# Experts on scaled f16 halves in place of fp32r halves, with range checks, wider weight pieces and work moved to GpSimd

## The chip, the cores and the metric

The kernel runs on one core of one Trainium2 chip. The metric is device time in microseconds. A core has TensorE (PE, its weight loads listed as PEld), VectorE (DVE), ScalarE (ACT), GpSimd (POOL), SyncE (SP, which only issues transfers here) and 16 DMA engines.

## The reference

Three parts follow one another. The first is bucketed attention: a query sees only the keys that have the same six sign bits. The second sends each of 1536 tokens to one of eight experts. The third is a dense layer pair with a hard gate.

```
q_bucket, k_bucket = six sign bits of q @ proj, k @ proj        # 16 heads, 768 positions, 64 wide
attn = softmax(where(q_bucket == k_bucket, q @ k.T / 8, -1e9))
x = (attn @ v) as 1536 tokens x 512
expert_idx = argmax(x @ w_gate); gate_w = its softmax value     # 8 experts, capacity 384 each
out[i] = gate_w[i] * (relu(x[i] @ w1[e]) @ w2[e])               # w1 512 x 1024, w2 1024 x 512
h = out @ w_in;  g = h * clip(h + 3, 0, 6) / 6                  # 512 -> 2048
result = g @ w_out                                              # 2048 -> 512
```

## The kernel before

The order of each engine's instructions is the order in which the Python code calls them; pools of buffers add the waits. Four stages stand one behind the other: attention, the routing with the first gather of tokens, the experts, and the last layer pair. Some work of the next stage is placed between the matmuls of the one that runs.

**Experts.** The loop in lines 1102 to 1148 runs over eight experts. Tokens of an expert are gathered from memory by POOL's queue into two tiles `xg` (`gather`, line 938), multiplied by their gate value (`scale_x`, line 945, DVE), transposed by PE and split by ACT and DVE into a high and a low half `xh`, `xl` (`make_x`, lines 954 to 958). An expert handles W = 224 columns of tokens. `gemm1` (line 971) has KF = 8 steps f of twelve matmuls: three products of halves (high with high, low with high, high with low) for four pieces of the inner dimension. ACT takes the high half of the result through Relu (`hh`, line 973), DVE the low one (`hl`, line 974). `gemm2` (line 997) has eight steps s of twelve matmuls; every second one ends with an eviction to `yTh` (ACT, line 1000) and `yTl` (DVE, line 1001), which are f16. All halves before that are fp32r. psh and psy have three PSUM buffers each.

**Weights.** `load_w` issues transfers of 512 KB on SP's queue into four buffers `rawp`. `split_w` halves them in pieces of 512 columns: `wh` on ACT (line 144), `wl` on DVE (line 145). Each expert has 16 such pieces; those of w2 are made in the steps of its own gemm1, those of w1 in the steps of the gemm2 ahead of it:

```
for f in range(KF):                                  # gemm1 of expert e
    split_w(wp2, e, 2 + f // 4, f % 4)
    if nxt and f % 2:
        load_w(e + 1, f // 4, (f // 2) % 2)
    gemm1(e, f)
    if 0 < e < 4:
        next(cgen, None)
    elif 3 < e < 7 and f % 2:
        zeros(4 * (e - 4) + f // 2)
```

**Beside them.** `compact` is a generator that computes indices with small DVE operations and a few matmuls; experts 1 to 3 take one item of it per step of gemm1. `zeros` (lines 981 and 983, ACT) writes zeros behind the tokens of each slot; experts 4 to 6 do four calls of two copies each. scale_x of the next expert stands at s = 2 and 3 of gemm2, make_x at s = 5 and 6.

**Last stage.** `up` (line 1190) and `down` (line 1217) work on f16 halves, the up weights being split into `ch` and `cl`. Sums of squares of the halves are collected through ACT's accumulator (line 1160), and `verdict` sets a flag when one of four sums is out of range; then a second branch computes the experts and the rest again in fp32. POOL scatters the result (line 1232).

Of the kernel before, what the change touches and what calls it, by code (L numbers as in the profile page):

```python
# [56 lines left out]
@with_exitstack
def moe_attention_kernel(ctx, tc, qk, v, vt, pj, wg, w1, w2, win, wout, out, cap):
# [43 lines left out]
    s8 = persist([P, 8], F32, "s8")  # L102
    f9 = persist([1, 9], F32, "f9")
# [20 lines left out]
    rawp = opened(wctx, "rawp", 4, side="right")  # L124
# [11 lines left out]
    def split_w(wp, e, i, q, lo=None):  # L136
        lo = lo or dve
        kind = "12"[i // 2]
        if q == 0:
            wh[e, i] = wp.tile([P, 2048], F32R, tag=f"wh{kind}", name=f"wh{e}_{i}")  # L140
            wl[e, i] = wp.tile([P, 2048], F32R, tag=f"wl{kind}", name=f"wl{e}_{i}")
        r = raw[e, i, q // 2][:, (q % 2) * 512 : (q % 2 + 1) * 512]
        c = slice(q * 512, (q + 1) * 512)
        act.activation(wh[e, i][:, c], r, AF.Copy)  # L144
        lo.tensor_tensor(out=wl[e, i][:, c], in0=r, in1=f32(wh[e, i])[:, c], op=ALU.subtract)  # L145
# [128 lines left out]
    with ExitStack() as actx:  # L274
# [668 lines left out]
    def scale_x(e, j):  # L943
        t = xg_t[e, j]
        dve.tensor_scalar(out=t, in0=t, scalar1=gates[:, e, j : j + 1], scalar2=None, op0=ALU.mult)

    def make_x(e, j):
        if j == 0:
            xs_t[e] = tuple(xp.tile([P, KD, W], F32R, tag=n, name=f"{n}{e}") for n in ("xh", "xl"))
        xh, xl = xs_t[e]  # L950
        t = xg_t.pop((e, j))
        ps = ps_a.tile([P, KD, P], F32, tag="a", name=f"psa{e}{j}")
        for k in range(KD):
            pe.transpose(ps[:, k], t[:, k * P : (k + 1) * P], ident)
        c = slice(j * GW, (j + 1) * GW)
        ps = ps[:, :, 0:GW]
        act.activation(xh[:, :, c], ps, AF.Copy)
        dve.tensor_tensor(out=xl[:, :, c], in0=ps, in1=f32(xh)[:, :, c], op=ALU.subtract)

    def gemm1(e, f):  # L960
        xh, xl = xs_t[e]
        if f == 0:
            h_t[e] = tuple(xp.tile([P, KF, W], F32R, tag=n, name=f"{n}{e}") for n in ("hh", "hl"))
# [9 lines left out]
        act.activation(hh[:, f], ps, AF.Relu)  # L973
        dve.scalar_tensor_tensor(out=hl[:, f], in0=ps, scalar=0.0, in1=f32(hh)[:, f], op0=ALU.max, op1=ALU.subtract)
# [12 lines left out]
    def gemm2(e, d, half, ra, rv):  # L987
# [114 lines left out]
    for e in range(E):  # L1102
# [45 lines left out]
    with ExitStack() as cctx:  # L1148
# [13 lines left out]
        def spans():  # L1162
            o = 2 * KG
            for i, (a, b) in enumerate(((0, o), (o, o + KG), (o + KG, o + 2 * KG), (o + 2 * KG, o + 2 * KG + KD))):
                dve.tensor_reduce(out=s8[:, i : i + 1], in_=sq[:, a:b], axis=AX.X, op=ALU.add)
            dve.tensor_scalar(out=s8[:, 4:8], in0=s8[:, 0:4], scalar1=TOP, scalar2=None, op0=ALU.is_le)

        def verdict():
            ps = ps_g.tile([P, 512], F32, tag="g", name="psr")
            pe.matmul(ps[0:1, 0:8], ones[:, 0:1], s8, start=True, stop=True)  # L1170
            for i, c in enumerate((LOW, P - 0.5)):
                t = slice(4 * i, 4 * i + 4)
                dve.tensor_scalar(out=f9[:, t], in0=ps[0:1, t], scalar1=c, scalar2=None, op0=ALU.is_lt)
            dve.tensor_copy(f9[:, 8:9], flag[0:1, E : E + 1])
            with nc.allow_low_precision("counts"):
                dve.tensor_reduce(out=redo, in_=f9, axis=AX.X, op=ALU.add)
# [236 lines left out]
```

## Time and profile before

| | us |
|---|---|
| median of 3 runs | 698.89 (697.9 to 699.05) |
| the profiled execution | 697.97 |
| span of its profile | 696.2 |
| mean granted TensorE clock | 0.976 of full speed |

The share of an engine's busy time is a mean over stages. The chain that ended last is followed back from the last instruction: every piece is a stretch in which the named work set the end. The attention lasts to about 240 us, the routing and the first gather to 254, the experts from 254.18 to 432.74, the last stage to about 670, and the scatters and the exit fill the rest.

### The profile page before, as it was taken

To read this page: it belongs to the slowest core of one execution; us is meant where nothing else is said; L and a number is where in the kernel's file an instruction comes from. 1 tells how busy PE (TensorE), PEld (TensorE's weight loads), DVE (VectorE), ACT (ScalarE), POOL (GpSimd) and SP (SyncE) were. 2 spreads that over 40 slices of the span, in tenths; PEclk is the share of its full clock that TensorE was granted. 3 is DMA by queue.
4 is the path that set the end of the run, shared out by engine and by line. 5 is a ranking of instruction groups with operands and counts; after the bars stand their busy time and mean duration, and the time that the engine had idled before them with its cause. 6 is when DMAs were issued, how large, how long until landed. Compare 5 with 4: busy or idle time off the path is not lost.

```text
span 696.2 us, 14332 instructions
## 1 busy us (share of the span) xinstructions
PE 662.7 (95%) x5518; PEld 504.7 (72%) x5518; DVE 487.7 (70%) x1030; ACT 436.6 (63%) x857; POOL 187.9 (27%) x154
## 2 busy tenths in 40 slices
PE   7999999999999689999999999999999999999894
PEld 2578889889888569999999999555555555555441
DVE  6767898898999878888777677788888532222320
ACT  3467878878788646566588763555455476556740
POOL 4338769769775131011100000000000011000011
PEclk8799999999999989999999999999999999999998
DMA  8584774774383086666666555344443001000011
GB/s 229 123 226 113 220 189 119 215 189 120 75 226 111 8 259 214 212 210 215 212 205 197 188 173 180 108 136 138 139 147 120 1 32 61 0 1 1 1 39 56
DMA packets 37841, 94.14 MB, mean 135 GB/s; under 512 B 7577, under 2 KB 13721, under 8 KB 37761
## 3 DMA queue, kind: packets, MB, share of 16 engines
q1 hardware_dynamic: 34672, 85.71, 41.9%
q0 software_dynamic: 2400, 7.36, 3.2%
q8 instruction: 46, 0.75, 0.5%
q14 instruction: 35, 0.28, 0.1%
q10 hardware_dynamic: 688, 0.03, 0.1%
HBM read 67.14 MB, written 6.29 MB: 105 GB/s over the span
## 4 chain that ended last, share of the span: by engine, by line
PE 78%; DVE 9%; DMA 6%; ACT 4%; issue 2%; SPq 0%; POOL 0%; POOLq 0%; ACTq 0%; DVEq 0%
PE psg L1190 16%; PE pso L1217 16%; PE psh L971 12%; PE psy L997 12%; PE psm L395 5%; PE pst L412 4%; PE pst L413 3%; DVE mx L398 2%; PE psv L440 2%; PE psv L441 2%; PE psv L442 2%; DMA out_dram<-os,inv 2%; PE psg L501 2%; DMA X<-b 1%; DVE vh L648 1%
## 5 line engine op out<-in xcount | busy, mean ns | idle before, releaser
L428 POOL TENSOR_TENSOR plo<-pf,phi 128x768 f16<-128x768 f32 x86 | 146.3, 1725 | 63.4 <-ACT phi L422 25.0
L414 ACT ACTIVATE pf<-pst 128x384 f32<-128x384 f32 x192 | 83.4, 486 | 50.4 <-PE pst L413 49.1
L398 DVE TENSOR_REDUCE mx<-psm 128x1 f32<-128x384 f32 x192 | 96.3, 548 | 19.7 <-PE psm L395 19.2
L145 DVE TENSOR_TENSOR wl<-raw,wh 128x512 fp32r<-128x512 f32 x128 | 86.5, 687 | 17.4 <-ACT wh L144 13.9
L1232 POOL DMA_INDIRECT out_dram<-os,inv x12 | 12.2, 1020 | 310.6 <-DVE os L1224 284.3
L1190 PE MATMUL psg<-yTh,ch 128*128 128x512 f16 (+1 forms) x256 | 83.4, 326 | 3.2 <-DVE rl L1193 3.2
L1190 PE MATMUL psg<-yTl,ch 128*128 128x512 f16 (+1 forms) x256 | 83.4, 326 | 0.0
L1190 PE MATMUL psg<-yTh,cl 128*128 128x512 f16 (+1 forms) x256 | 83.4, 326 | 0.0
L1193 DVE SCALAR_TENSOR_TENSOR rl<-rl,psg 128x512 f32<-128x512 f32 x64 | 35.0, 551 | 66.6 <-ACT rl L1192 66.2
L144 ACT ACTIVATE wh<-raw 128x512 fp32r<-128x512 f32 x128 | 77.2, 622 | 1.2 <-issue 0.6
L412 PE MATMUL pst<-Y,K 128*128 128x384 f32 x192 | 74.7, 389 | 2.0 <-ACT pf L414 2.0
L1190 PEld LDWEIGHTS <-ch 128*128 128x128 f16 x512 | 50.1, 98 | 35.9
L422 ACT ACTIVATE phi<-pf 128x768 f16<-128x768 f32 x85 | 71.7, 843 | 1.9
L395 PE MATMUL psm<-K,X 76*128 76x384 f32 x192 | 67.1, 430 | 6.0 <-DVE mx L398 4.5
L1217 PE MATMUL pso<-ch,gh 128*128 128x512 f16 x192 | 72.8, 379 | 0.0
L1217 PE MATMUL pso<-ch,gl 128*128 128x512 f16 x192 | 72.8, 379 | 0.0
L1217 PE MATMUL pso<-cl,gh 128*128 128x512 f16 x192 | 72.8, 379 | 0.0
L997 PE MATMUL psy<-hh,wh 128*128 128x224 f32 x256 | 71.3, 279 | 0.0
L997 PE MATMUL psy<-hh,wl 128*128 128x224 f32 x256 | 70.3, 274 | 0.0
L997 PE MATMUL psy<-hl,wh 128*128 128x224 f32 x256 | 70.1, 274 | 0.0
L1217 PEld LDWEIGHTS <-gh 128*128 128x128 f16 x384 | 37.6, 98 | 42.3
L413 PE MATMUL pst<-X,K 77*128 77x384 f32 x192 | 66.2, 345 | 0.0
(211 smaller groups left out, 1558.9 us busy)
## 6 DMA issues: line engine op xcount, KB each, us to landing
raw<-in_w_dram SPq DMA_DIRECT2D x64, 512.0 KB
rc<-in_win_dram SPq DMA_DIRECT2D x16, 512.0 KB
rc<-in_wout_dram SPq DMA_DIRECT2D x16, 512.0 KB
r<-in_qk_dram SPq DMA_DIRECT2D x16, 384.0 KB
K<-hi SPq DMA_DIRECT2D x31, 192.0 KB
vr<-in_v_dram SPq DMA_DIRECT2D x4, 768.0 KB
vt<-in_vt_dram SPq DMA_DIRECT2D x8, 384.0 KB
Y<-hi SPq DMA_DIRECT2D x16, 192.0 KB
```

The costliest lines, as they stand in the source:

```text
L144: act.activation(wh[e, i][:, c], r, AF.Copy)
L145: lo.tensor_tensor(out=wl[e, i][:, c], in0=r, in1=f32(wh[e, i])[:, c], op=ALU.subtract)
L395: pe.matmul(ps[:, :HS], st["X"][0:76, c::NC], st["K2"][0:76, n * HS : (n + 1) * HS], start=True, stop=True)
L398: dve.tensor_reduce(out=mm[:, c, n : n + 1], in_=ps[:, :HS], axis=AX.X, op=ALU.max)
L412: pe.matmul(ps[:, :HS], st["K1"][:, kc], st["Y"][:, qc], start=True, stop=False)
L413: pe.matmul(ps[:, :HS], st["K2"][0:77, kc], st["X"][0:77, qc], start=False, stop=True)
L414: act.activation(pf.rearrange("k (c n p) -> k c n p", c=NC, n=2)[:, :, n], ps[:, :HS].rearrange("k (p c) -> k c p", c=NC), AF.Exp, scale=0 ...
L428: eng.tensor_tensor(out=plo_t[k], in0=pf_t.pop(k), in1=phi_t[k], op=ALU.subtract)
L971: pe.matmul(ps, l[:, c], r[:, k], start=n == 0, stop=n == 3 * KD - 1)
L997: pe.matmul(ps, l, r, start=n == 0, stop=n == 3 * KF - 1)
L1190: pe.matmul(ps, l, x, start=n == 0, stop=n == 3 * KD - 1)
L1217: pe.matmul(po[blk][s], l, r, start=first and n == 0, stop=last and n == 2)
```

## The change

The halves of the experts' inputs, weights and hidden values become f16. They are multiplied by powers of two (SX = 2^9 for inputs, S1 = 2^7 and S2 = 2^8 for the weights), and the eviction to yTh and yTl divides these out. A matmul of f16 has a separate weight load in PE's program; the count and shape of the matmuls is the same.

Weights are split in pieces of 1024 columns inside the loop, of 512 ahead of it: the high half on ACT at even steps (`high_w`), the low half on DVE one step later (`low_w`), as a scalar_tensor_tensor that also writes a sum through its accumulator. hh writes a sum too, and `sample` takes squares of 128 columns of each weight half. In the last stage `ranges` turns these sums into values that `verdict` compares with thresholds, 28 in one comparison. scale_x runs on POOL except for expert 0, and the zero copies run on POOL. rawp has six buffers. `compact` is spread over experts 1 to 6, and its three operations that make `zoff` come first. The constant lines and the plain declarations are left out here:

```diff
-    rawp = opened(wctx, "rawp", 4, side="right")
+    rawp = opened(wctx, "rawp", 6, side="right")
...
+    def high_w(wp, e, i, c, n):
+        if c == 0:
+            wh[e, i] = wp.tile([P, 2048], F16, tag=f"wh{kind}", name=f"wh{e}_{i}")
+            wl[e, i] = wp.tile([P, 2048], F16, tag=f"wl{kind}", name=f"wl{e}_{i}")
+        r = raw[e, i, c // 1024][:, c % 1024 : c % 1024 + n]
+        act.activation(wh[e, i][:, c : c + n], r, AF.Copy, scale=(S1, S2)[i // 2])
+        late.append((e, i, c, n, r))
+
+    def low_w():
+        while late:
+            e, i, c, n, r = late.pop(0)
+            dve.scalar_tensor_tensor(
+                out=wl[e, i][:, c : c + n], in0=r, scalar=(S1, S2)[i // 2], in1=wh[e, i][:, c : c + n],
+                op0=ALU.mult, op1=ALU.subtract, accum_out=wlo[:, nlo[0] : nlo[0] + 1],
+            )
+            nlo[0] += 1
+
+    def sample(e, i):
+        t = wh[e, 2 * i][:, 0:P]
+        act.activation(wj, t, AF.Square, accum_out=wsq[:, 2 * e + i : 2 * e + i + 1])
...
+            dve.tensor_copy(vsc[:, g : g + 1], sc[:, 0:1])
...
-        dve.tensor_scalar(out=t, in0=t, scalar1=gates[:, e, j : j + 1], scalar2=None, op0=ALU.mult)
+        eng = pool if e else dve
+        eng.tensor_scalar(
+            out=t, in0=t, scalar1=gates[:, e, j : j + 1], scalar2=1.0, op0=ALU.mult, op1=ALU.mult
+        )
...
-        act.activation(xh[:, :, c], ps, AF.Copy)
-        dve.tensor_tensor(out=xl[:, :, c], in0=ps, in1=f32(xh)[:, :, c], op=ALU.subtract)
+        act.activation(xh[:, :, c], ps, AF.Copy, scale=SX)
+        dve.scalar_tensor_tensor(out=xl[:, :, c], in0=ps, scalar=SX, in1=xh[:, :, c], op0=ALU.mult, op1=ALU.subtract)
...
-        act.activation(hh[:, f], ps, AF.Relu)
+        i = e * KF + f
+        act.activation(hh[:, f], ps, AF.Relu, accum_out=hsum[:, i : i + 1])
...
-        rz = act.value_load(zoff[0:1, i : i + 1], min_val=0, max_val=YW - P)
+        rz = pool.value_load(zoff[0:1, i : i + 1], min_val=0, max_val=YW - P)
         for t in (yTh, yTl):
-            act.activation(t[:, :, ds(rz, P)], mid(zt, KD), AF.Copy)
+            pool.tensor_copy(t[:, :, ds(rz, P)], mid(zt, KD))
...
-            act.activation(yTh[:, d, ds(ra, W)], ps, AF.Copy, scale=SY)
+            c = SY / (SX * S1 * S2)
+            act.activation(yTh[:, d, ds(ra, W)], ps, AF.Copy, scale=c)
...
         for f in range(KF):
-            split_w(wp2, e, 2 + f // 4, f % 4)
-            if nxt and f % 2:
+            low_w()
+            if f % 2 == 0:
+                high_w(wp2, e, 2 + f // 4, 512 * (f % 4), 1024)
+            elif nxt:
                 load_w(e + 1, f // 4, (f // 2) % 2)
             gemm1(e, f)
-            if 0 < e < 4:
+            if f % 4 == 3:
+                sample(e, f // 4)
+            if 0 < e < 7:
                 next(cgen, None)
-            elif 3 < e < 7 and f % 2:
-                zeros(4 * (e - 4) + f // 2)
+                if e > 3 and f % 2:
+                    zeros(4 * (e - 4) + f // 2)
...
         for s in range(KF):
+            low_w()
             if nxt:
-                split_w(wp1, e + 1, s // 4, s % 4)
-                if s % 2:
+                if s % 2 == 0:
+                    high_w(wp1, e + 1, s // 4, 512 * (s % 4), 1024)
+                else:
                     load_w(e + 1, 2 + s // 4, (s // 2) % 2)
...
+        def ranges():
+            dve.tensor_reduce(out=sv[:, 4:5], in_=hsum, axis=AX.X, op=ALU.add)
+            for i, (t, lo, hi) in enumerate(
+                ((wlo[:, : nlo[0]], -TALL, TALL), (hsum, -1.0, TALL), (vsc, 2.0**9, 2.0**24))
+            ):
+                k = wok[:, : t.shape[-1]]
+                dve.tensor_scalar(out=k, in0=t, scalar1=hi, scalar2=None, op0=ALU.is_le)
+                dve.scalar_tensor_tensor(out=k, in0=t, scalar=lo, in1=k, op0=ALU.is_ge, op1=ALU.mult)
+                dve.tensor_reduce(out=sv[:, 25 + i : 26 + i], in_=k, axis=AX.X, op=ALU.add)
```

DVE, the first four steps of gemm1 in expert 5 (hl is the low half of the hidden values, wl that of w2, raw the loaded weights). Before:

```order
L145 TENSOR_TENSOR wl_2_6850<-raw_2_0_6710,wh_2_6849 128x512 [waits DMAHW7_49,Activation_49]
L974 SCALAR_TENSOR_TENSOR hl_6854<-psh_6855,hh_6853 128x224 [waits Activation_49]
L145 TENSOR_TENSOR wl_2_6850<-raw_2_0_6710,wh_2_6849 128x512 [waits Activation_49]
L974 SCALAR_TENSOR_TENSOR hl_6854<-psh_6874,hh_6853 128x224 [waits Activation_49]
L145 TENSOR_TENSOR wl_2_6850<-raw_2_1_6744,wh_2_6849 128x512 [waits DMAHW0_49,Activation_49]
L974 SCALAR_TENSOR_TENSOR hl_6854<-psh_6902,hh_6853 128x224 [waits Activation_49]
L145 TENSOR_TENSOR wl_2_6850<-raw_2_1_6744,wh_2_6849 128x512 [waits Activation_49]
L974 SCALAR_TENSOR_TENSOR hl_6854<-psh_6921,hh_6853 128x224 [waits Activation_49]
```

and now:

```order
L1010 SCALAR_TENSOR_TENSOR hl_6793<-psh_6794,hh_6792 128x224 [waits Activation_49]
L163 SCALAR_TENSOR_TENSOR wl_2_6790,wlo<-raw_2_0_6656,wh_2_6789 128x1024 [waits DMAHW7_49]
L1010 SCALAR_TENSOR_TENSOR hl_6793<-psh_6812,hh_6792 128x224 [waits Activation_49]
L1010 SCALAR_TENSOR_TENSOR hl_6793<-psh_6839,hh_6792 128x224 [waits Activation_49]
L163 SCALAR_TENSOR_TENSOR wl_2_6790,wlo<-raw_2_1_6688,wh_2_6789 128x1024 [waits DMAHW0_49]
L1010 SCALAR_TENSOR_TENSOR hl_6793<-psh_6857,hh_6792 128x224 [waits Activation_49]
L1010 SCALAR_TENSOR_TENSOR hl_6793<-psh_6887,hh_6792 128x224 [waits Activation_49]
L163 SCALAR_TENSOR_TENSOR wl_3_6885,wlo<-raw_3_0_6722,wh_3_6884 128x1024 [waits DMAHW1_49]
```

Eight rows of 512 and 224 columns in turn were one pair per step; now a row of 1024 stands between every second pair of hl, and its wait for ACT has gone into an earlier row.

POOL, from gemm2 of expert 4 to expert 5 (xg are gathered tokens, zt is a tile of zeros). Before, the gathers alone:

```order
L938 DMA xg_6475<-xd,ids 128x512 [waits DMASW7_49,DVE_49,PE_49]
L938 DMA xg_6477<-xd,ids 128x512 [waits DMASW0_49,DVE_49,PE_49]
L938 DMA xg_6845<-xd,ids 128x512 [waits DMASW1_49,DVE_49,PE_49]
L938 DMA xg_6847<-xd,ids 128x512 [waits DMASW2_49,DVE_49,PE_49]
L938 DMA xg_7215<-xd,ids 128x512 [waits DMASW3_49,DVE_49,PE_49]
```

and now, from scale_x for expert 5 on:

```order
L978 TENSOR_SCALAR xg_6785<-xg_6785,gates 128x512 [waits DMASW1_49]
L978 TENSOR_SCALAR xg_6787<-xg_6787,gates 128x512 [waits DMASW2_49]
L970 DMA xg_7141<-xd,ids 128x512 [waits PE_49]
L970 DMA xg_7143<-xd,ids 128x512 [waits PE_49]
L1017 TENSOR_LOAD zoff
L1017 ISA x2
L1019 ISA
L1019 COPY yTh<-zt 128x4x128 [waits DVE_49,Pool_49]
L1019 ISA
L1019 COPY yTl<-zt 128x4x128 [waits Pool_49]
```

The gathers, which had waited for DVE, stand behind scale_x on their own queue, and the register loads and copies of zeros behind them.

SP, the loads of the first two experts' weights behind the write of xd, the tokens. Before:

```order
L482 DMA xd<-xp_4379 768x1x128 [waits DMAHW6_49,DVE_49,Activation_49]
L131 DMA raw_2_0_5088<-in_w_dram 128x1024 [waits DMAHW7_49]
L131 DMA raw_2_1_5090<-in_w_dram 128x1024 [waits DMAHW0_49]
L131 DMA raw_3_0_5092<-in_w_dram 128x1024 [waits DMAHW1_49,DVE_49]
L131 DMA raw_3_1_5094<-in_w_dram 128x1024 [waits DMAHW3_49,DMAHW2_49,DVE_49]
L131 DMA raw_0_0_5130<-in_w_dram 128x1024 [waits DMAHW7_49,DMAHW3_49,DVE_49]
```

and now:

```order
L512 DMA xd<-xp_4389 768x1x128 [waits DMAHW6_49,DVE_49,Activation_49]
L143 DMA raw_2_0_5099<-in_w_dram 128x1024 [waits DMAHW7_49]
L143 DMA raw_2_1_5101<-in_w_dram 128x1024 [waits DMAHW0_49]
L143 DMA raw_3_0_5103<-in_w_dram 128x1024 [waits DMAHW1_49]
L143 DMA raw_3_1_5105<-in_w_dram 128x1024 [waits DMAHW2_49]
L143 DMA raw_0_0_5139<-in_w_dram 128x1024 [waits DMAHW3_49,DVE_49]
```

Four loads stand there now without a wait for DVE, where two did.

## Rows read from the trace of the kernel before

**Rows 1.** The page, busy time (share of the span) and instructions by engine.

```profile
PE 662.7 (95%) x5518; PEld 504.7 (72%) x5518; DVE 487.7 (70%) x1030; ACT 436.6 (63%) x857; POOL 187.9 (27%) x154
```

**Rows 2.** Chain that ended last, experts: start, duration (us), engine, name, line, count.

```profile
276.89 10.72 PE psh L971 x96
...
295.65 0.44 PE psa L954 x4
...
299.19 10.72 PE psh L971 x96
...
422.02 10.72 PE psy L997 x96
432.74 3.93 PE psg L1190 x24
```

**Rows 3.** Windows, 290 to 310: busy per engine (count), TensorE clock, DMA share, GB/s.

```profile
290.00:310.00 20.00, 20.00 (x182) 20.00 (x181) 16.21 (x37) 12.36 (x28) 1.89 (x2) 1.00 0.67 216
```

**Rows 4.** PE's timeline, last stage and attention, and weight loads by form (busy, mean ns).

```profile
449.14 0.38 PE L1190 MATMUL psg<-yTh,ch 128*128 128x512 f16 x1
...
451.73 0.27 PE L1190 MATMUL psg<-yTh,ch 128*128 128x256 f16 x1
...
452.17 0.27 PE L1190 MATMUL psg<-yTh,cl 128*128 128x256 f16 x1
...
139.55 0.20 PE L440 MATMUL psv<-vh,phi 128*128 128x73 f16 x1
...
140.00 0.20 PE L441 MATMUL psv<-vh,phi 128*128 128x72 f16 x1
...
L1190 PEld LDWEIGHTS <-ch 128*128 128x128 f16 x512 | 50.1, 98 | 35.9
```

**Rows 5.** Timelines of DVE and ACT in an expert: start, duration, form [idle before].

```profile
396.76 0.69 DVE L145 TENSOR_TENSOR wl<-raw,wh 128x512 fp32r<-128x512 f32 x1 [0.77 <-ACT wh L144]
397.37 0.38 DVE L974 SCALAR_TENSOR_TENSOR hl<-psh,hh 128x224 fp32r<-128x224 f32 x1
397.67 0.68 DVE L145 TENSOR_TENSOR wl<-raw,wh 128x512 fp32r<-128x512 f32 x1
...
396.11 0.61 ACT L144 ACTIVATE wh<-raw 128x512 fp32r<-128x512 f32 x1
396.63 0.34 ACT L973 ACTIVATE hh<-psh 128x224 fp32r<-128x224 f32 x1
396.87 0.62 ACT L144 ACTIVATE wh<-raw 128x512 fp32r<-128x512 f32 x1
```

**Rows 6.** Groups by form, last stage: busy us, mean ns | idle before, releaser.

```profile
L1201 DVE SCALAR_TENSOR_TENSOR gl<-rl,gh 128x768 f16<-128x768 f32 x32 | 30.7, 958 | 29.1 <-ACT gh L1200 29.1
...
L1160 ACT ACTIVATION_READ_ACCUMULATOR junk<-gh 128x1 f32 x32 | 6.0, 186 | 0.0
```

**Rows 7.** Timelines of DVE and POOL in attention, and a memset by form.

```profile
125.55 0.95 DVE L345 SCALAR_TENSOR_TENSOR lo<-r,hi 128x768 fp32r<-128x768 f32 x1
...
191.68 2.06 DVE L345 SCALAR_TENSOR_TENSOR lo<-r,hi 128x768 fp32r<-128x768 f32 x1
...
191.27 1.66 POOL L428 TENSOR_TENSOR plo<-pf,phi 128x768 f16<-128x768 f32 x1 [0.51 <-POOL plo L428]
...
L658 POOL MEMSET fill<- 1x768 f32 x1 | 0.7, 730 | 0.1
```

**Rows 8.** Chain that ended last, from the routing to the first expert.

```profile
242.86 4.28 DMA raw<-in_w_dram
247.13 5.13 DMA xg<-xd,ids x2
...
254.18 1.60 PE psh L971 x12
```

**Rows 9.** Windows, 244.5 to 250.5, columns as in group 3.

```profile
244.50:248.00 3.50, 2.97 (x14) 1.21 (x12) 2.93 (x15) 1.70 (x4) 1.38 (x2) 0.50 0.92 312
248.00:250.50 2.50, 2.36 (x14) 1.10 (x13) 1.75 (x5) 0.00 (x0) 1.89 (x3) 0.63 0.51 143
```

More of the change, by code (lines that the diff above doesn't have):

```diff
@@ L48 @@
 EPS = 1e-9
+SX = 2.0**9
+S1 = 2.0**7
+S2 = 2.0**8
 SY = 2.0**17
@@ L53 @@
 TOP = 3.7e9
+TALL = 6.0e4
 LOW = float(NT * DF)
+NSPLIT = 2 * E * 4096 // 512
+NV = 28
 @with_exitstack
@@ L101, in moe_attention_kernel @@
     sq = persist([P, 2 * KG + 2 * KG + KD], F32, "sq")
-    s8 = persist([P, 8], F32, "s8")
-    f9 = persist([1, 9], F32, "f9")
+    sv = persist([P, NV], F32, "sv")
+    thr = persist([1, NV], F32, "thr")
+    bad = persist([1, NV + 1], F32, "bad")
+    wlo = persist([P, NSPLIT], F32, "wlo")
+    wok = persist([P, NSPLIT], F32, "wok")
+    wsq = persist([P, 2 * E], F32, "wsq")
+    hsum = persist([P, E * KF], F32, "hsum")
+    vsc = persist([P, NH // 4], F32, "vsc")
     redo = persist([1, 1], I32, "redo")
@@ L134, in moe_attention_kernel, with split_w @@
     wh, wl = {}, {}
-    def split_w(wp, e, i, q, lo=None):
-        lo = lo or dve
+    nlo = [0]
+    late = []
+    def high_w(wp, e, i, c, n):
         kind = "12"[i // 2]
[L139 to L145, printed above, removed]
+        if c == 0:
[12 more added lines that the diff above has]
+            nlo[0] += 1
+    def split_w(wp, e, i, q):
+        high_w(wp, e, i, 512 * q, 512)
+        low_w()
+    def sample(e, i):
+        t = wh[e, 2 * i][:, 0:P]
+        act.activation(wj, t, AF.Square, accum_out=wsq[:, 2 * e + i : 2 * e + i + 1])
     NE = B * NC
@@ L868, in compact @@
         so = so_t[0]
+        z = rtile([NS], "z")
+        dve.tensor_scalar(out=z, in0=iota_s, scalar1=float(P), scalar2=so[:, E : E + 1], op0=ALU.mult, op1=ALU.add)
+        yield
+        dve.tensor_scalar(out=z, in0=z, scalar1=float(YW - P), scalar2=None, op0=ALU.min)
+        yield
+        dve.tensor_copy(zoff, z)
+        yield
         o2 = oh.rearrange("p b c e -> p (b c) e")
@@ L972, in gemm1 @@
                 n += 1
-        act.activation(hh[:, f], ps, AF.Relu)
-        dve.scalar_tensor_tensor(out=hl[:, f], in0=ps, scalar=0.0, in1=f32(hh)[:, f], op0=ALU.max, op1=ALU.subtract)
+        i = e * KF + f
+        act.activation(hh[:, f], ps, AF.Relu, accum_out=hsum[:, i : i + 1])
+        dve.scalar_tensor_tensor(out=hl[:, f], in0=ps, scalar=0.0, in1=hh[:, f], op0=ALU.max, op1=ALU.subtract)
     zt = yp.tile([P, P], F16, tag="zt", name="zt")
@@ L999, in gemm2 @@
         if half:
-            act.activation(yTh[:, d, ds(ra, W)], ps, AF.Copy, scale=SY)
+            c = SY / (SX * S1 * S2)
+            act.activation(yTh[:, d, ds(ra, W)], ps, AF.Copy, scale=c)
             dve.scalar_tensor_tensor(
-                out=yTl[:, d, ds(rv, W)], in0=ps, scalar=SY, in1=yTh[:, d, ds(rv, W)], op0=ALU.mult, op1=ALU.subtract
+                out=yTl[:, d, ds(rv, W)], in0=ps, scalar=c, in1=yTh[:, d, ds(rv, W)], op0=ALU.mult, op1=ALU.subtract
             )
@@ L1168, in verdict @@
         def verdict():
             ps = ps_g.tile([P, 512], F32, tag="g", name="psr")
[L1170 to L1174, printed above, removed]
+            pe.matmul(ps[0:1, 0:NV], ones[:, 0:1], sv, start=True, stop=True)
@@ L1262, in moe_attention_kernel @@
         for m in range(TOT + 2):
+            if m == KG + 2:
+                ranges()
             if m == KG:
```

32 lines of the change are left out of this document (19 added, 13 removed).

## The prediction

> **What bounds the kernel now.** I read the busy line first: TensorE (PE) is busy for 95% of the span, the other engines for 70% or less [rows 1]. That is an average over four stages, so the chain of work that ended last comes next, in the stretch of the experts. There it is matmuls without a gap: 96 of gemm1 take 10.72 us, the 96 of gemm2 take as long, and two groups of four transposes 0.44 us each [rows 2]. From one gemm1 to the next it is 299.19 − 276.89 = 22.30 us; eight experts fill 254.18 [rows 8] to 432.74 [rows 2]. The busy times in a window inside the stage say the same: PE 20.00 of 20.00 us, VectorE (DVE) 16.21, ScalarE (ACT) 12.36, GpSimd (POOL) 1.89, DMA share 0.67, clock 1.00 [rows 3], which is the higher of TensorE's two levels, 2.4 GHz. So a faster matmul shows in the time at once, until DVE is the bound: it has 22.30 × (1 − 0.81) = 4 us of room per expert. Before the stage the bound is another: the chain goes over weight loads and the first expert's gather (242.86 to 247.13 + 5.13 = 252.26 [rows 8]), where the clock is at the lower level, 0.50 [rows 9].
>
> **The matmuls.** Their number stays: 12 per step × 16 steps × 8 experts = 1536, and 224 columns each. Only the type changes, from fp32r to f16. Before, one takes 10.72 / 96 = 0.1117 us [rows 2]. No f16 matmul of 224 columns is in the trace, but the last stage has f16 ones with the same 128x128 weights: twelve of 512 columns from 449.14 to 451.73 are 0.216 us apart, four of 256 columns from 451.73 to 452.17 are 0.110 apart [rows 4]. Scaled to 224 columns these give 0.0944 and 0.0963; I take 0.096, since 256 is the nearer. The saving is (0.1117 − 0.096) × 1536 = **24.1 us**. An upper end of the saving is 0.0944: 26.6 us. The lower end comes from the weights: f16 brings a separate weight load in front of every matmul, and such a load of 128x128 shows 98 ns [rows 4]. If a matmul could not follow faster than its load, 0.098 would leave 21.0 us. I do not take it, because the attention's matmuls of 72 and 73 columns, each with a load of its own (5518 loads for 5518 matmuls [rows 1]), are (140.00 − 139.55) / 13 = 0.035 us apart [rows 4], far below the duration of a load. A rule speaks against this part: the Trainium skill, "TensorE: Matmul & The Clock Gate", section "LDWEIGHTS (loading the stationary operand)", puts a load at its columns over 1.2 in nanoseconds, 107 for 128 columns, and if loads came one behind the other the sum would save 0.005 × 1536 = 7.7 us instead. Both the 98 ns and the 0.035 us spacing stand against it here.
>
> An expert's period becomes 192 × 0.096 + 2 × 0.44 = 19.3 us. The transposes stay in fp32 and keep 0.44.
>
> **Does DVE keep up in 19.3 us?** Starts of successive rows give what one costs when the engine has more to do: a low half of 512 columns 397.37 − 396.76 = 0.61, an hl of 224 columns 0.30 [rows 5]; 0.31 us for 288 columns more, or 1.08 ns per column. A piece of 1024 is then 0.61 + 512 × 0.00108 = 1.16. It becomes a scalar_tensor_tensor, and that form without an accumulator runs 768 columns in 958 ns [rows 6], no slower per column. Per expert: 8 pieces 9.3, 8 hl 2.4, 4 yTl 1.2, 2 xl of 448 columns 1.1; together 14.0. What the accumulator adds on DVE no row shows. Below, nothing; above, by the nearest row, ACT's read of its accumulator at 186 ns [rows 6], 8 × 0.19 = 1.5. The index work of `compact` is now spread over experts 1 to 6 at about one small operation per step, 1 us per expert. So 14 to 16.5 of 19.3: tighter than before, but not the bound. Two scale_x of 512 columns leave it.
>
> **ACT**, the same way: high half of 512 columns 396.63 − 396.11 = 0.52, hh 0.24 [rows 5], so 1.02 per piece of 1024 and 8 × 1.02 + 8 × 0.24 + 4 × 0.24 + 2 × 0.46 = 12.0; with 8 reads of hh's accumulator and two small samples 13 to 14.3. Not the bound. The zero copies leave it. Both engines' work on a step ends inside the next: psh and psy have three buffers, so a late eviction has two steps of 1.15 us before PE waits. Hence the accumulators and samples cost 0.
>
> **POOL's new work.** scale_x (two per expert) and, in experts 4 to 6, eight zero copies move to POOL. Their duration there is not in the trace. A memset of 768 columns, with no input, takes 0.73 us, and plo, with two inputs and 768 columns, 1.66 [rows 7]. For 512 columns that is 0.49 to 1.11, or up to 1.7 if width does not help; I take 0.8. POOL was nearly idle here (1.89 of 20 us) [rows 3], so its time costs nothing by itself. Its price is on DVE: the operation `lo` (two inputs in SBUF) takes 0.95 us alone, but 2.06 when it starts 0.41 us into POOL's plo, and it ends 0.81 us after that one [rows 7]. It waited for POOL. Of the experts' DVE work only the weight pieces have two SBUF inputs (hl, yTl and xl read PSUM). A piece that meets a 0.8 us copy loses 0.4 on average. In experts 4 to 6 four to six pieces may meet one: 2 us per expert against 3 us of room. Behind a waiting piece stands hl, which the next gemm needs, with two steps of slack. I put **+0.7 us** on it in all; ends 0 and +4 (every room used up in three experts).
>
> **Before the first expert.** rawp grows from 4 to 6 buffers, and SP's rows there lose a wait: four loads of 512 KB go out together where two went. Before, transfers ran at 312 GB/s (share 0.92) from 244.5 to 248, and the gather's data came alone behind them at 143 GB/s [rows 9]. This gather ends at 252.26 on the chain [rows 8]. One more MB at 312 GB/s is 3.4 us. If it delays the gather in full, +3.4; if the gather's rows keep their place among 16 engines that are half idle from 248, 0. I take **+1.0**, since the gather alone left half of the DMA time free.
>
> **The rest at nothing.** The four vsc copies hide beside attention's PE work. `ranges` adds some eleven tiny DVE operations and seven memsets in the last stage, whose DVE mostly waits for ACT (29.1 us idle before gl alone [rows 6]); without that cover 2 us. The step from gemm2 to the last stage stays as it is, as does everything behind it. Freed weight space decides no transfer on the chain.
>
> **Sum.** The profiled execution took 697.97 us, 0.9 less than the median of the runs (698.89). 697.97 − 24.1 + 1.0 + 0.7 = 675.6; between the two bases, **676 us**. Ends: 697.97 − 26.6 = 671.4 and 698.89 − 21.0 + 3.4 + 4 = 685.3.
>
> **Rivals.**
> *POOL comes too late.* In experts 4 to 6, scale_x of the next expert stands behind eight copies and four register loads on POOL. Its transposes are due after 13 of 16 steps, some 16 us after gemm1 began, and the first yTh and yTl (ACT, DVE) now wait for the copies at 11.5 us, with psy's three buffers as slack to 16. At 0.8 us a copy POOL is done at 10; it decides from about 1.4 us a copy. At 1.7 us, plo's duration, the transposes would be some 3 us late in three experts: +9, **685 us**. For it: plo's 1.66. Against: a copy has one input of f16.
>
> *DVE becomes the bound: slower than before.* If the accumulating form of scalar_tensor_tensor ran at half rate, a piece would take 2 × 1.16 and its read 0.19 more, 2.4 to 2.5 us: 8 × 2.45 + 4.7 + 1 = 25.3 us per expert for seven, over 22.3. That is 7 × 25.3 + 13 = 190 against 178.6 before: **about 709 us**. Nothing is lost below (19.3 − 5.7) / 8 = 1.7 us a piece; slower than before from about 2.1. Against: gl runs this operation at full rate [rows 6], and ACT's accumulator costs a separate short read, not a slower pass.
>
> *Weight loads bare.* If each matmul also had to wait for its weights, because loads of neighbouring f16 matmuls do not overlap as they do in attention, the spacing is at least 0.098: **679 us**, inside the range. At the page's 107 ns it would be 692.
>
> *It does not do what it says:* a check of the value ranges fails on these inputs, and the fp32 branch runs the experts again, by 178 us at least: over 850.
>
> **How the numbers follow.** Forecast 0.80; POOL late 0.11; bare loads 0.04, slow accumulator 0.03, the branch 0.01, something unnamed near no change 0.01. The range is 672 to 683: it leaves out half of POOL's case and the last two. About 0.2% (1.4 us) is what a measurement of this kernel can tell from no change: faster 0.95, same 0.01, slower 0.04.
>
> **What would show it.** Right: in the profile after, 96 matmuls of gemm1 in the chain take 9.2 us, a period of 19.3, PE still at 1.00 in the stage; weight pieces of 1024 columns at about 1.2 us on DVE with a busy time under 17 of 20; POOL copies under 1 us; the first gemm1 at 254 to 257; the last stage as long as before. Wrong: gaps before transposes or psy in experts 4 to 6 that end with POOL (late); DVE pieces of 2 us and more with PE waiting for weights; a matmul spacing of 0.107; the gather ending past 256.

## The result

The changed kernel takes 675.42 us (median of four, 674.08 to 677.99) against 698.39 for the kernel before: a ratio of 0.9687, 95% interval 0.964 to 0.9734. The forecast was 676.0 with a range of 672 to 683. The profiled execution took 675.88 us; 697.97 − 675.88 = 22.1 us are to be found in the trace.

The page of the kernel after, as [rows 1]:

```profile
span 674.1 us, 14367 instructions
...
PE 638.4 (95%) x5518; PEld 479.7 (71%) x5518; DVE 481.0 (71%) x1038; ACT 426.6 (63%) x869; POOL 229.8 (34%) x199
```

The shares of the engines are almost what they were; only POOL's grew. The chain that ended last, from the routing to the last stage (start, duration, engine, name, line, count), as [rows 2, 8]; gemm1, the gather and the first gemm1 have other lengths than before:

```profile
240.87 4.73 DMA raw<-in_w_dram
...
247.42 5.70 DMA xg<-xd,ids
...
255.04 2.02 PE psh L1006 x12
...
257.09 9.00 PE psh L1006 x84
...
276.25 9.20 PE psh L1006 x96
...
292.35 0.44 PE psa L989 x4
...
295.53 9.20 PE psh L1006 x96
...
410.90 3.91 PE psg L1249 x24
```

96 matmuls of gemm1 take 9.20 us where they took 10.72, and from one gemm1 to the next it is 295.53 − 276.25 = 19.28 us where it was 22.30. The transposes still take 0.44. Ahead of that, two rows are longer than before: the gather lands at 253.12, and the first gemm1 needs 2.02 + 9.00 us, almost 2 us more than the later ones.

Inside the stage the windows show PE still without a gap, at clock 1.00 (columns as in [rows 3]). The second window lies in the experts with zero copies:

```profile
290.00:310.00 20.00, 20.00 (x210) 19.98 (x208) 16.83 (x42) 14.47 (x36) 4.33 (x4) 1.00 0.77 249
350.00:370.00 20.00, 20.00 (x210) 19.98 (x208) 16.68 (x31) 13.84 (x35) 12.77 (x12) 1.00 0.77 245
```

The chain lets the time be split by stage. The stages are read from the starts of PE rows (the last of psv, attention's output; the first of psh, gemm1's result; the first of psg on yTh, with which the last stage begins):

| | before | after | difference |
|---|---|---|---|
| to attention's last matmul | 239.89 | 237.90 | −1.99 |
| from there to the first expert's gemm1 | 14.29 | 17.14 | +2.85 |
| eight experts | 178.39 | 155.70 | −22.69 |
| last stage to the end of the span | 263.62 | 263.36 | −0.26 |

The sum is −22.09. The first row can't be put down to the change, which adds only a few small operations there: over the fourteen profiles of this case attention's last matmul of scores (pst) starts anywhere between 231.8 and 235.1 us, in two profiles of one and the same kernel (f16_only, below) at 231.8 and 234.0, and the difference is there in full at about 66 us. The last row scatters by 2 us as well. Single executions of a kernel that ran nine times differ by 4 to 6 us in all, so the experiments below are read by stage first.

### The profile page after: what moved, and what is told of

It is laid out like the page before. It is cut to its first block, busy times and chain, and to the rows that moved or that the text cites. A ratio compares the mean times of both kernels' runs of the same rounds, so it can differ in the third digit from the quotient of the medians.

```text
span 674.1 us, 14367 instructions
## 1 busy us (share of the span) xinstructions
PE 638.4 (95%) x5518; PEld 479.7 (71%) x5518; DVE 481.0 (71%) x1038; ACT 426.6 (63%) x869; POOL 229.8 (34%) x199
## 4 chain that ended last, share of the span: by engine, by line
PE 75%; DVE 10%; DMA 6%; ACT 5%; issue 2%; SPq 0%; POOL 0%; POOLq 0%; ACTq 0%; DVEq 0%
PE psg L1249 16%; PE pso L1276 15%; PE psh L1006 11%; PE psy L1033 11%; PE psm L425 5%; PE pst L442 4%; PE pst L443 3%; DVE mx L428 2%; DMA out_dram<-os,inv 2%; PE psv L470 2%; PE psv L471 2%; PE psv L472 2%; PE psg L531 2%; DMA vr<-in_v_dram 1%; ACT junk L1203 1%
## 5 line engine op out<-in xcount | busy, mean ns | idle before, releaser
L1291 POOL DMA_INDIRECT out_dram<-os,inv x12 | 12.1, 1008 | 270.8 <-DVE os L1283 244.5
L163 DVE SCALAR_TENSOR_TENSOR wl<-raw,wh 128x1024 f16<-128x1024 f32 (+1 forms) x68 | 82.7, 1218 | 6.3 <-ACT wh L157 5.2
L157 ACT ACTIVATE wh<-raw 128x1024 f16<-128x1024 f32 (+1 forms) x68 | 67.6, 999 | 0.5 <-issue 0.4
L1033 PE MATMUL psy<-hh,wl 128*128 128x224 f16 x256 | 66.3, 259 | 0.0
L1033 PE MATMUL psy<-hh,wh 128*128 128x224 f16 x256 | 66.3, 259 | 0.0
L1033 PE MATMUL psy<-hl,wh 128*128 128x224 f16 x256 | 66.3, 259 | 0.0
```

Source lines behind the costliest of these rows:

```text
L163: dve.scalar_tensor_tensor(out=wl[e, i][:, c : c + n], in0=r, scalar=(S1, S2)[i // 2], in1=wh[e, i][:, c : c + n], op0=ALU.mult, op1=ALU.s ...
L1033: pe.matmul(ps, l, r, start=n == 0, stop=n == 3 * KF - 1)
```

## The experiments

One table for all, from the same rows. Experts are numbered from 0, as in the code; a is the time from attention's last matmul to the first gemm1. Two numbers in a column of one time are two profiles of the same kernel; of experts 4 to 6, those with the zero copies, the first profile's are given. The median is that of all timed executions:

| kernel | a | expert 0 | experts 4, 5, 6 | eight experts | median us |
|---|---|---|---|---|---|
| before | 14.29 | 22.54 | 22.31, 22.31, 22.31 | 178.39 | 697.62 |
| after | 17.14, 15.56 | 21.05, 21.06 | 19.57, 19.27, 19.37 | 155.70, 155.61 | 675.18 |
| late_loads | 14.63, 14.25 | 19.42, 19.41 | 19.57, 19.27, 19.38 | 154.07, 153.96 | 674.91 |
| heat | 17.49 | 19.79 | 19.57, 19.27, 19.38 | 154.44 | 676.13 |
| raw4 | 13.70, 13.80 | 19.80, 19.86 | 19.57, 19.27, 19.37 | 154.45, 154.41 | 674.99 |
| f16_only | 14.05, 14.39 | 19.32, 19.32 | 19.82, 19.82, 19.82 | 155.68, 155.67 | 673.10 |
| zeros2 | 16.30 | 22.11 | 21.43, 20.96, 20.95 | 161.92 | 680.86 |
| low15 | 16.81 | 23.52 | 23.31, 22.17, 22.64 | 176.77 | 697.14 |
| no_pool | 15.01 | 21.06 | 21.11, 21.10, 21.10 | 160.79 | 681.64 |
| no_sums | 16.40 | 21.73 | 19.57, 19.27, 19.27 | 156.07 | 674.16 |

**f16_only: is the gain the matmuls' spacing alone?** The kernel before, with types and scales changed and nothing else (DVE's tensor_tensor becomes a scalar_tensor_tensor where it has to scale):

```diff
-            wh[e, i] = wp.tile([P, 2048], F32R, tag=f"wh{kind}", name=f"wh{e}_{i}")
+            wh[e, i] = wp.tile([P, 2048], F16, tag=f"wh{kind}", name=f"wh{e}_{i}")
...
-        act.activation(wh[e, i][:, c], r, AF.Copy)
+        act.activation(wh[e, i][:, c], r, AF.Copy, scale=k)
```

(the same for wl, xh, xl, hh and hl)

> The kernel before with only the types and scales of the experts' halves changed to f16: pieces of 512, DVE's scale_x, ACT's zeros, four buffers, no sums, no range checks. Theory (the whole gain is the matmul's spacing, 0.1117 to 0.0958, and everything else costs or gives nothing there): 698.4 - 24.2 = 674.2, with a period of 19.3 us; without the late gather of after it may be lower than after by up to 4, so 671 to 674. Rival (the other parts are needed to feed PE in 19.3 us, since ACT would be busy for 12.4 / 20 x 22.3 = 13.8 us, and 4.9 more in the experts with zeros, and takes part in every step): gaps in PE in experts 4 to 6, a gain of 15 to 20, about 680.

673.05 us at first, and once more beside the kernel after:

> The same kernel as f16_only. Its profile showed 14.05 + 155.68 = 169.7 us for that stretch, 3.1 less than after; its median of four was 673.05. Theory: 672.3, so that the change without its other parts is 3 us faster than with them. Rival: 675.4, the same as after.

673.73 us (672.25 to 675.75). So the types alone carry all of the gain. Over nine executions each its mean is 673.8 and that of after 675.5, with standard deviations of 1.7 and 1.6: 1.7 ± 1.6 us better than after, where a and the eight experts together were 3.1 and 1.1 us shorter in the two pairs of profiles. That the other parts cost something is likely, how much the total does not settle. The rival is there in small: in experts 4 to 6 the period is 19.82, not 19.27. (Expert 3 takes 19.94, but it took 22.88 against 22.31 before: matmuls of `compact` lie in it.) A window and the chain in expert 5 show who ends it:

```profile
350.00:370.00 20.00, 19.88 (x204) 19.42 (x203) 15.90 (x34) 17.33 (x39) 0.00 (x0) 1.00 0.75 243
...
352.97 0.61 ACT yTl L989
353.58 0.52 ACT wh L148
354.11 0.23 ACT hh L979
```

PE has small gaps, and on the chain lie ACT's rows one behind the other: the second zero copy, a weight piece, hh. ACT is at 17.33 of 20 us there.

**no_pool: what does the move to POOL do?** scale_x back on DVE, the zero copies back on ACT:

```diff
-        eng = pool if e else dve
+        eng = dve
...
-        rz = pool.value_load(zoff[0:1, i : i + 1], min_val=0, max_val=YW - P)
+        rz = act.value_load(zoff[0:1, i : i + 1], min_val=0, max_val=YW - P)
-            pool.tensor_copy(t[:, :, ds(rz, P)], mid(zt, KD))
+            act.activation(t[:, :, ds(rz, P)], mid(zt, KD), AF.Copy)
```

> The kernel after with scale_x back on DVE and the zero copies back on ACT. Theory (POOL was no bound and its lock with DVE cost nothing on the chain): the weight pieces of 1024 columns fall from a mean of 1.29 to 1.23 us or less, and the time stays within 1 us of after, 674.4 to 676.4, unless ACT gets full in experts 4 to 6 (14.5 of 20 us busy plus 8 x 0.61 = 4.9: 19.4 of 20): then +1 to +5 there. Rival (the lock held DVE up): 1 to 3 us faster.

681.64 us (679.57 to 682.86): 6 us slower than after. The expectation's condition came true: experts 4 to 6 take 21.1 us, 5.1 us more in all, and nothing else in the stage changed. The window of one of them and the chain through its gemm1:

```profile
350.00:370.00 20.00, 18.84 (x191) 18.08 (x189) 14.15 (x31) 17.21 (x41) 1.89 (x2) 1.00 0.71 225
...
359.20 0.76 ACT wh L157
...
362.14 0.45 ACT wh L157
...
363.03 0.73 ACT hh L1009 x4
363.76 0.52 ACT yTh L1019
364.28 0.52 ACT yTl L1019
364.80 0.74 ACT wh L157
...
365.61 0.15 ACTq L1017
```

POOL has no copy left, PE waits for 1.2 us of 20, and from 357.4 to 366.1 the chain runs along ACT without a break. DVE's pieces fall to a mean of 1.22 us as expected, but that buys nothing, since DVE was not the bound. So of the parts beside the types, this one is needed. Over its whole period ACT would have room: in expert 5 it is busy for 17.61 us, less than 19.3. But the copies all stand in gemm1, and there two steps take ACT 362.14 − 359.20 = 2.94 and 364.80 − 362.14 = 2.66 us, where PE needs 2 × 1.15 = 2.30. f16_only has its copies on ACT too, without sums and samples, and loses 0.55 us per expert by them, no_pool 1.83. That the sums, samples and wider pieces make the difference fits, but no run has them taken away with the copies on ACT.

**no_sums: do the sums cost?** No accumulator on wl and hh, no samples, no ranges:

```diff
-            act.activation(hh[:, f], ps, AF.Relu, accum_out=hsum[:, i : i + 1])
+            act.activation(hh[:, f], ps, AF.Relu)
...
-            if m == KG + 2:
-                ranges()
```

(and the comparisons of before in `verdict`)

> The kernel after without the experts' sums and samples (no accumulator on wl and hh, no squares of weights), without ranges, with the old two comparisons in verdict. Theory (they lie beside PE): within 1 us of after. Rival (the reads and the eleven operations in the last stage cost up to 2 us): 673.4.

674.16 us (673.22 to 676.1), and by stage 156.07 against 155.70 for the experts. Without expert 0, which is the subject of the next experiments, it is 134.34 against 134.65. Nothing that the total can tell, as the theory had it.

**late_loads, heat, raw4: where do 2.9 us ahead of the experts and 1.8 in the first gemm1 come from?** In after two more loads of 512 KB go out ahead of the gather. (xd is the copy of the tokens in memory from which the gather reads; `heat` issues idle matmuls, whose results nobody reads, so that PE keeps running.) Windows of after, moved by the 2 us by which it is ahead, so that they answer to [rows 9]; the last lies in the first gemm1:

```profile
242.50:246.00 3.50, 2.83 (x11) 1.21 (x12) 2.93 (x15) 1.70 (x4) 0.71 (x2) 0.50 0.95 302
246.00:248.50 2.50, 2.36 (x12) 1.01 (x11) 1.77 (x7) 0.00 (x0) 2.20 (x2) 0.50 1.02 408
248.50:253.00 4.50, 1.82 (x9) 0.73 (x7) 0.55 (x1) 0.54 (x1) 1.98 (x3) 0.98 0.88 293
256.00:258.00 2.00, 2.00 (x14) 1.61 (x13) 1.52 (x8) 1.41 (x4) 1.61 (x2) 0.50 0.05 12
```

From 246 to 248.5 weight loads alone fill all engines at 408 GB/s, and the gather's first packet starts at 248.53; before, in the same place, the gather was nearly alone with a share of 0.51 and 143 GB/s [rows 9]. The gather's data land 253.12 − 240.28 = 12.84 us after the write of xd was issued, before 252.26 − 242.26 = 10.0. Then PE, which has run out of idle matmuls, stands still, and in the first gemm1 the granted clock is 0.50, the lower level. late_loads takes the two loads out of the way:

```diff
+    for q in range(2):
+        load_w(0, 2, q)
     gather(0)
...
     for j in range(2):
         make_x(0, j)
+        if j == 0:
+            load_w(0, 3, 0, act)
+            load_w(0, 3, 1, act)
...
-    for q in range(4):
-        load_w(0, 2 + q // 2, q % 2)
```

(on ACT's queue; the other two loads stay on SP's)

> The kernel after, with the last two loads of the first expert's w2 (1 MB) issued on ACT's queue behind the first xh instead of on SP's queue ahead of the gather. Theory (the loads collide with the gather, and the idle PE loses clock): the data of the second gather land about 10 us after the write of xd is issued, as before the change, not 12.8; the first gemm1 runs at clock 1.00 in 9.3 us, not 11.0; about 671 us, 4 less than after. Rival (the gather is late for another reason, such as POOL's own issue): no change, 675. A second rival: the loads come too late for the steps from 4 on of the first expert, and PE waits there instead: 675 or more.

Its chain and the window in the first gemm1:

```profile
248.78 3.69 DMA xg<-xd,ids
...
254.39 1.31 PE psh L1006 x12
...
255.73 8.07 PE psh L1006 x84
...
256.00:258.00 2.00, 2.00 (x24) 2.00 (x22) 1.52 (x6) 1.72 (x6) 0.79 (x2) 1.00 0.96 389
```

The gather lands 10.3 us after xd's write and the first gemm1 takes 1.31 + 8.07 = 9.4 us at clock 1.00: both steps of the theory hold. The total did not show it, 675.46 us from four executions, and the repeat was put beside after itself:

> The same kernel as late_loads. Its profile showed 14.63 + 154.07 = 168.7 us for that stretch, 4.1 less than after, and its median of four 675.46 did not show it. Theory (the rest of that run was noise): 671.3. Rival (moving the loads costs elsewhere what it gains here): 675.4.

> The kernel after, unchanged, once more beside the three others of this call, since single executions differ by up to 4 us in the first 66 us of attention and in the last scatters, and four of them were not enough to see 4 us. From attention's last matmul to the last stage it took 17.14 + 155.70 = 172.8 us. Expected: 675.4 (674.4 to 676.4).

Here late_loads took 672.54 (671.68 to 675.41) and after 675.18 (673.57 to 678.02). Over nine executions each the means are 674.5 and 675.5, 1.1 ± 1.6 us apart. The stages show 3.5 us (means of the two profiles of each, a and eight experts together); the profiled executions of late_loads lost 2 to 3 us in attention, ahead of the edit. Whether all of the 3.5 reaches the total is open.

heat leaves the loads where they are and keeps PE running:

```diff
-    heat(HT[1])
+    heat(HT[1] + 7)
...
         make_x(0, j)
+        if j == 0:
+            heat(6)
```

> The kernel after, with seven more idle matmuls behind the second gather's index work and six between the two groups of transposes of expert 0, so that PE runs until its next work. Theory (the first gemm1 is slow only since PE stood idle before it): the gather ends as late as in after (12.8 us behind xd), but the clock is 1.00 in gemm1, 9.3 instead of 11.0 us: about 673.7. Rival (gemm1 waits for split weights or loads, the clock only reflects that): 11 us again, 675.4 or a little more.

Its PE rows between the two groups of transposes, and a window in the first gemm1:

```profile
252.88 1.46 PE L1085 MATMUL heat<-ohr,ident 128*128 128x512 f16 x6
254.18 0.60 PE L989 MATMUL psa<-ident,xg 128*128 128x128 f32 x4
...
257.00:259.00 2.00, 2.00 (x23) 2.00 (x21) 1.52 (x6) 1.72 (x6) 1.46 (x2) 1.00 0.44 74
```

The clock is 1.00, the first gemm1 takes 9.25 us from its first matmul to that of gemm2, as in late_loads, where after needs 10.88, and expert 0 falls from 21.05 to 19.79. So the slow first gemm1 is a matter of the clock alone. DVE starts on the second tile of the gather 11.95 us after the write of xd was issued, earlier than the expectation had it, but later than in the second profile of after (11.28), whose clock fell too. The six idle matmuls stood in the way of the second group of transposes, which were held from 252.88 to 254.18; a is 17.49, and the total is 676.13, no better than after.

raw4 undoes the two buffers:

```diff
-    rawp = opened(wctx, "rawp", 6, side="right")
+    rawp = opened(wctx, "rawp", 4, side="right")
```

> The kernel after with four buffers for raw weights instead of six. Theory: SP's third and fourth load wait for DVE again, the gather ends about 10 us behind xd, the first gemm1 takes 9.3 us, and in the loop four buffers do, since a load then has some six steps of 1.15 us to land: about 671. Rival (the two buffers are needed at 19.3 us per expert): gaps in PE that end with a DMA or with wh and wl, 675 to 685.

```profile
246.61 3.10 DMA xg<-xd,ids
...
252.10 1.31 PE psh L1006 x12
...
272.07 9.20 PE psh L1006 x96
```

The gather takes 3.10 us on the chain instead of 5.70, the first gemm1 starts 13.70 us after attention, and all later periods are the same as with six buffers. The rival falls: the two buffers feed nothing that was hungry. 675.28 us at first; once more:

> The same kernel as raw4. Its profile showed 13.70 + 154.45 = 168.15 us for that stretch, 4.7 less than after; its median of four was 675.28. Theory: 670.7. Rival: 675.3.

674.21 (673.0 to 675.36). By stage it is 3.8 us shorter than after, by the nine totals each 0.7 ± 1.7.

The fourteen profiles agree on both steps. In the seven with four loads ahead of the gather (after twice, heat, zeros2, low15, no_pool, no_sums) its first packet starts 8.1 to 8.7 us after the write of xd was issued, in the seven others 6.2 to 7.1. And in the first gemm1 the granted clock is at 0.50 for a while in those seven, heat excepted, and in none of the others. How late the data are varies: DVE starts on the second tile 12.87 us behind xd in the first profile of after, 10.7 to 11.95 in the six others of its kind, and 9.4 to 10.4 in the seven with two loads.

No version here beats after by a difference that its totals can tell, except f16_only, just, which leaves out the range checks.

**zeros2 and low15: do the two rivals of the prediction exist, and from where on?** The zero copies twice:

```diff
             pool.tensor_copy(t[:, :, ds(rz, P)], mid(zt, KD))
+            pool.tensor_copy(t[:, :, ds(rz, P)], mid(zt, KD))
```

> The kernel after with each zero copy on POOL made twice, 16 in each of experts 4 to 6. After shows 0.61 us for a copy alone and 1.60 for one that meets a weight piece on DVE, 7.5 us for eight, and POOL done 6.7 us ahead of the transposes' due time less the 3.3 of scale_x. Theory (POOL's deadline, the rival of the prediction): sixteen take about 15 us, scale_x then ends some 4 us behind the transposes' due time, PE waits in three experts: +12, about 687, the gaps ending with POOL. Against it (copies do not set an end, or most of the extra ones run beside DVE work that has room): within 2 us of after.

680.86 us (two executions). What PE waited for in the stage (us in total, times, longest), and POOL's first copy and its scale_x for the next expert:

```profile
PE psa L989 <- POOL xg L978: 4.4, 3, 1.6
...
358.11 0.61 POOL L1019 COPY yTh<-zt 128x512 f16 x1 [0.73 <-DVE yTl L1039]
...
372.80 2.32 POOL L978 TENSOR_SCALAR xg<-xg,gates 128x512 f32<-128x512 f32 x2
```

Sixteen copies take 372.80 − 358.11 = 14.7 us, as expected; PE then waits for scale_x, once in each of three experts. The periods grow by 1.9, 1.7 and 1.6, 5.1 in all, not 12. The expectation had let the first transposes wait for both scale_x of 1.67 us each; they wait for the first alone, which takes 0.69 of the 2.32 us. In after, expert 5's copies end at 363.30 and the transposes start at 369.79: less 0.69 that is 5.8 us of room, and 14.7 − 7.5 = 7.2 us of copies more leave 1.4, which is most of what was measured. The mechanism is there, its price was too high.

Half of each low piece made twice, on DVE:

```diff
+            if n == 1024:
+                dve.scalar_tensor_tensor(
+                    out=wl[e, i][:, c : c + 512], in0=r[:, 0:512], scalar=(S1, S2)[i // 2],
+                    in1=wh[e, i][:, c : c + 512], op0=ALU.mult, op1=ALU.subtract,
+                )
```

> The kernel after with half of each weight piece's low half made twice on DVE (60 more scalar_tensor_tensor of 512 columns). By the prediction's price a piece then costs 1.23 + 0.08 + 0.61 = 1.9 us, above the 1.7 from which DVE should be the bound: 8 x 1.9 + 4.7 + 1 = 20.9 us per expert, 1.6 over 19.3 in seven experts: +11, about 686, with POOL's copies adding up to 5 more in experts 4 to 6. Against it (slack elsewhere takes it up): within 2 us of after.

697.14 us (695.57 to 699.31), and so the whole gain is gone. What PE waits for, two pieces of the chain (the new rows have line 168), and the window:

```profile
PE psy L1038 <- DVE wl L168: 8.9, 8, 1.6
PE psh L1011 <- DVE hl L1015: 8.5, 14, 1.4
...
286.57 1.15 DVE wl L163 x2
...
287.74 1.05 DVE wl L168
...
289.72 1.15 DVE wl L163 x2
...
290.90 0.69 DVE wl L168
...
350.00:370.00 20.00, 16.82 (x172) 16.22 (x170) 19.14 (x35) 11.42 (x29) 12.73 (x11) 1.00 0.66 217
```

Two DVE rows hold PE up, and DVE is busy for 19.14 of 20 us. The direction was right, the price too low: a piece with its repeat lasts between 290.90 + 0.69 − 289.72 = 1.87 and 287.74 + 1.05 − 286.57 = 2.22 us, where 1.9 was set down, and experts 1 to 6 take 21.5 to 23.3 us, not 20.9.

## Why the prediction was right, step by step

**The matmuls.** Right, and the whole of the gain. The spacing is 9.20 / 96 = 0.0958 us; 0.096 was taken from the f16 matmuls of 256 and 512 columns [rows 4]. The stage's saving by it is (0.1117 − 0.0958) × 1536 = 24.4 us. The weight loads show 98 ns and do not set the spacing: the 0.098 of the lower end is above what was measured. The Trainium skill ("TensorE: Matmul & The Clock Gate", "LDWEIGHTS (loading the stationary operand)") puts a load at its columns over 1.2 in nanoseconds, by estimate 107 here; the rows have 98, and the measurement decides. The trace of before could have said as much: the profile lists a load beside every fp32r matmul as well (5518 of each [rows 1]), nearly twice as long, and there too it set no spacing. So in this profile a load per matmul is nothing that f16 brings. First before, then after (busy us, mean ns):

```profile
L971 PEld LDWEIGHTS psh<-xh,wl 128*128 128x128 f32 x256 | 33.7, 192 | 0.0
...
L1033 PEld LDWEIGHTS <-wh 128*128 128x128 f16 x512 | 49.6, 98 | 0.0
```

**DVE and ACT keep up.** Right. DVE is busy for 16.83 of 20 us, which is 16.2 of a period of 19.3 (14 to 16.5 were set down); ACT for 14.47, which is 14.0 (13 to 14.3). The unknown was the accumulator on DVE, bounded by 0 and 0.19 us:

```profile
L163 DVE SCALAR_TENSOR_TENSOR wl<-raw,wh 128x1024 f16<-128x1024 f32 x60 | 77.1, 1286 | 6.2 <-ACT wh L157 5.2 <-ACT yTh L1037 0.7
...
L1009 ACT ACTIVATION_READ_ACCUMULATOR hh<-psh 128x1 f32 x64 | 12.6, 197 | 0.0
...
L163 DVE DVE_READ_ACCUMULATOR wl<-raw,wh 128x1 f32 x68 | 5.5, 81 | 0.0
```

The read shows 0.08 us, and even that is no loss: in expert 5 the read and the row behind it both start at 355.00, 1.14 us after their piece, and without a read, in no_sums, it is 1.13. On ACT a read of 0.19 us holds the next row up by 0.09:

```profile
356.45 0.19 ACT L1009 ACTIVATION_READ_ACCUMULATOR hh<-psh 128x1 f32 x1
356.54 1.05 ACT L157 ACTIVATE wh<-raw 128x1024 f16<-128x1024 f32 x1
```

A piece lasts 1.22 us alone, and the slower rival (2.4 to 2.5 us) was far off; low15 shows that pieces of 1.9 to 2.2 us already cost the whole gain, a little earlier than the prediction's 2.1.

**POOL.** The price of +0.7 us was too high: PE waits for nothing of POOL's, DVE's pieces or ACT's between the first expert and the last stage. The one row of what PE waited for there is the step to the last stage:

```profile
PE psg L1249 <- DVE rl L1252: 0.6, 2, 0.5
```

The lock itself is as [rows 7] had it, in both directions (DVE's, then POOL's timeline in expert 5):

```profile
353.86 1.22 DVE L163 SCALAR_TENSOR_TENSOR wl<-raw,wh 128x1024 f16<-128x1024 f32 x1
...
355.87 1.65 DVE L163 SCALAR_TENSOR_TENSOR wl<-raw,wh 128x1024 f16<-128x1024 f32 x1
...
355.84 0.61 POOL L1019 COPY yTh<-zt 128x512 f16 x1 [6.27 <-DVE yTl L1038]
356.40 1.60 POOL L1019 COPY yTl<-zt 128x512 f16 x1
```

A piece that meets a copy takes 1.65 us instead of 1.22, and a copy that meets a piece 1.60 instead of 0.61. Eight copies take 363.30 − 355.84 = 7.46 us, 0.93 each, where 0.8 was set down. All of it lies in the room that both have (DVE busy for 16.68 of 20 us in that window, POOL for 12.77). The working left out a part of the question, though: it asked what the copies cost on POOL, not what they would cost where they were. no_pool gives the answer for this kernel, 5 us; in f16_only it is 3 × 0.55 = 1.65.

**Before the first expert.** The mis-sized term. +1.0 was taken between 0 and 3.4; the profile shows +2.85, the second profile of after +1.3, three other kernels with the same loads 16.30 to 16.81 us for a, about +2.2, and no_pool +0.7 (there the clock had fallen before attention ended, and a starts later). The reasoning "the gather alone left half of the DMA time free" was wrong in that the two loads took all of it, at 408 GB/s, ahead of the gather.

**The first gemm1.** A term that the sum did not have. The late gather leaves PE without work, the clock goes to 0.50, and expert 0 takes 21.05 us where 19.42 (late_loads) is possible: +1.6. [Rows 9] could have raised the question: they show PE at the lower level shortly ahead of the first gemm1 before the change, but the prediction only used them for the transfers.

**The sum.** −24.4 for the matmuls, +1.6 for the clock, +0.1 for small things give the stage's −22.7; with +2.85 ahead of it the change itself brings about 19.8 us in the profiled pair, and 2.2 more lie in attention and in the end, where executions scatter. Against the 22.4 of the sum, the mis-sized and the missing term make 3.5 us, and POOL's 0.7 and the matmuls' 0.3 go the other way. In the second profile of after the same two stages give 1.27 − 22.78 = −21.5. The medians, 698.39 and 675.42, are 23.0 apart, those of all executions of the table 22.4. So the number came out nearer than its terms deserve, and that part is luck: the terms were off by 0.3 to 1.9 us each, inside the bounds that the range had been given, and the scatter of attention made up for them. The prediction's 1.4 us for what a measurement can tell from no change was too fine as well: the interval of the ratio, 0.964 to 0.9734, is ±3.3 us wide.

**The rivals.** POOL late, bare loads and the slow accumulator did not occur; the range checks did not send the kernel into its second branch. zeros2 and low15 show that the first and the third exist: POOL sets the end at 1.84 us per pair of copies (14.7 / 8), by 1.6 to 1.9 us per expert, so by an estimate from (7.5 + 5.8) / 8 = 1.7 us on (1.4 was predicted); DVE does at pieces of 1.9 to 2.2.

## What to carry to other kernels

When one engine's work per period becomes shorter, set every other engine's work against the new length, with and without each part that the change moves away, and do it for each stretch of the period by itself: the copies that were free on ACT at 22.3 us would still fit into 19.3, but not into the gemm1 in which they stand, and back there they cost 5 us. A deeper pool of buffers does not only help the loop that it was meant for; it also lets loads start earlier at the loop's entry, and there one must look at which transfer on the chain they meet and what PE does while it waits. Where executions of a kernel scatter by 2 us, stage times of two profiles tell a change of 3 us apart long before the totals do.

## What the runs showed of the hardware

- fp32r matmuls of 224 columns are 0.1117 us apart, f16 ones 0.0958; the loads beside them, 192 and 98 ns each, are hidden.
- The read of an accumulator shows 81 ns on DVE and 197 on ACT; the next row starts with it on DVE (355.00) and 0.09 us behind its start on ACT (356.45, 356.54).
- A GpSimd copy of 128x512 in f16 takes 0.61 us alone and 1.60 when a DVE operation with two inputs in SBUF runs. The Trainium skill ("SBUF — State Buffer", "Who interferes with whom") says that a DVE instruction with two SBUF inputs contends with a GpSimd instruction that reads SBUF, over a shared port that works as an exclusive lock; the rows agree: the copy loses 0.99 us, most of a piece of 1.22, and the piece 0.43, most of a copy of 0.61.
- In after PE was busy for 1.82 of 4.5 us ahead of the first gemm1 and had clock 0.50 in it; late_loads, with the gather earlier, and heat, with idle matmuls in that place, had 1.00.
